# Six plain units for nine in a gated product, eight decoded blocks in the experts, and a ranking matmul placed later

## The chip, the cores and the metric

The kernel runs on one core of one Trainium2 chip. The time is the device time of one launch in microseconds (us). A core has a tensor engine (TensorE, PE), three engines for elementwise work (VectorE = DVE, ScalarE = ACT, GpSimd = POOL), an engine that issues most DMA transfers (SyncE, SP), and 16 DMA engines. Each engine works through a list of its own in order; semaphores tie the lists together.

## The reference

Three layers in a row, on 4 x 576 = 2304 tokens of 512 numbers:

```python
# 1: causal attention, 4 batches x 8 heads, 576 tokens, head dim 64
scores = q @ k.T / 8;  cum = cumsum(max(s, 0))
scores = where(causal, -1e9, scores + min(-(cum_i - cum_j), 0))
x = softmax(scores) @ v                    # -> [2304, 512]
# 2: mixture of experts, one expert for each token, D = 512, F = 1024, E = 8
expert_idx = argmax(x @ w_gate, 1);  gate_w = softmax prob of that expert
out[mask] = gate_w[mask, None] * (max(x[mask] @ w1[e], 0) @ w2[e])
# 3: RMS norm and a gated product, d_ff = 1536
xn = x / sqrt(mean(x * x) + 1e-6) * rms_g
g = xn @ w_gate;  y = (g * sigmoid(g) * (xn @ w_val)) @ w_out
```

The inputs w_gate, w_val and w_out of the third layer arrive as 64-bit numbers, all others as fp32.

## The kernel before

**Order.** PE, ACT, DVE and SP run their instructions in the order in which the program writes them. So what is written ahead of an instruction on the same engine also holds it up.

**Attention.** 16 pairs of heads, written by a plan of times (ten to a pair). For each batch `route(b)` scores the tokens, picks their experts and ranks them within their expert, as a generator that is advanced a step at a time between the pieces of attention. Its ranking matmuls (L509, L511: the triangle `tri` and the ones against the one-hot matrix `oh`, which DVE makes at L503) are put off by a number of steps for each batch, `(3, 10, 3, 0)[b]`. The tokens are then scattered to DRAM (`xs`) by GpSimd, ordered by expert.

**Experts.** `moe` runs experts 0 to 7. Expert 0 begins while the last batch is still being ranked: its first 256 rows go through `gemm1` and `gemm2` as transposed tiles; 128 rows more, the late rows `xl`, are loaded, multiplied by their gate weight (`gate`, L867 on ACT), turned by PE (`turn_tile`, `xq`, L894) and go through `rows_gemm1` (L973) and `rows_gemm2` (L984). Then `finish` norms the rows, and PE turns the late rows' result (`yt`, L1001). Weights come in pieces of 512 KB: `feed` takes the next item of the list `k.order` and issues its load on SP (L729) into a ring of four staging buffers; `split` takes the oldest loaded piece, makes its upper part on ACT (L744) and its remainder on DVE (L757), and feeds the next item. The list holds 56 pieces (experts 1 to 7, eight each) and, at every ninth place from 12 on, five *words*: blocks of 512 KB of 64-bit numbers, three of w_out and one each of w_gate and w_val. `decode_words` turns a word into fp32: two steps on DVE (L1239, L1240), the absolute value on ACT, then two more steps on DVE, then a store to DRAM on SP (`keep_words`, L786: `wo32`, `wg32`) and the feed of the next item. One word is decoded in each of experts 1 to 5, its first half behind column 0 of `gemm2`, its second half ahead of the add of column 1.

**Gated product.** 36 units (p, f): a pair of token groups p of 3 and a block f of 12 of the width 1536. A unit is a 2 x 2 block product. The plain units (`PLAIN`, nine of them: f = 0, 1, 2 for each p) use eight products of blocks; the other 27 use seven, with sums of the x blocks (`x_sum`, S1 to S4), sums of the weight blocks (`w_sum`) and more steps at the eviction (STEPS7 against STEPS8). A product is six matmuls of 384 columns (L1314, 2 halves x 3 passes of upper parts and remainders). All of it is written by times in units of a product: `SLOTS_V` and `SLOTS_G` are places on DVE and POOL, `fill` takes the next free one, `x_rests`, `x_sums`, `w_made` and `w_split` place the making of x and weight blocks. `glu_head` loads the first blocks during the last expert; the fp32 words of f = 0 are read back into `k.flat`. The second product (with w_out) follows.

```python
for n, item in enumerate(words):
    k.order.insert(WORDS_AT + 9 * n, item)
...
gemm2(k, 0, 1, NA)
rank(1)
gate(k, k.xl, ((0, 128),))
gemm2(k, 0, 2, NA)
...
turn_tile(k, k.xl[:, 0, :], *xb)
```

## Time and profile before

| | value |
|---|---|
| three timed runs, us | 848.29, 848.42, 849.98 (median 848.42) |
| profiled execution, us | 841.21, its span 839.5 |
| PE busy | 818.7 us, 98% |
| PE weight loads (beside PE) | 748.2 us, 89% |
| DVE busy | 640.0 us, 76% |
| ACT busy | 462.7 us, 55% |
| POOL busy | 226.5 us, 27% |
| granted clock of PE, mean | 0.994 |
| DMA | 146.72 MB, 175 GB/s |

On PE the stages lie thus in the span: attention to 184 us (the first `gemm1` matmul), the experts to 416 (the first of L1314), the gated product to 691, the second product to 828. On the other engines they overlap. Busy times are of one profiled execution, whose own time is 7.2 us below the median of the timed runs. A busy share is a mean over stages with different limits, so what an engine costs is read from who waits for whom in a stage.

### The profile page before, as it was taken

Reading aid. Unit: us, or ns where it says so; the run is one execution under the profiler, and the core shown is the slowest. Engines: PE = TensorE matmul, PEld = TensorE weight load, DVE = VectorE, ACT = ScalarE, POOL = GpSimd, SP = SyncE. Lnnn points to the kernel's source line nnn. Section 1 sums busy time; section 2 is a strip of 40 time slices with the busy share of each in tenths; the row PEclk is TensorE's granted clock in tenths of the full one; section 3 lists DMA queues with packets and bytes.
Section 4 is the critical chain, followed back from the end, with each engine's and each line's share of the span. In section 5 each row is a group of like instructions: output and inputs, shape, how many; then the busy total and the mean of one; then the engine's idle time right before and its main releaser. Section 6 shows DMA issues by size and latency. Waiting matters only on the chain.

```text
span 839.5 us, 15787 instructions
## 1 busy us (share of the span) xinstructions
PE 818.7 (98%) x5622; PEld 748.2 (89%) x5622; DVE 640.0 (76%) x1425; ACT 462.7 (55%) x1060; POOL 226.5 (27%) x249
## 2 busy tenths in 40 slices
PE   7999999999999999999999999999999999999994
PEld 4777767789899999999999999999999998899994
DVE  6557688965767767867698988888898969868880
ACT  5988988875756566566453443333333335453440
POOL 3335845342000000000131232544343352032120
PEclk9999999999999999999999999999999999999997
DMA  7999978246567576767651433323233375344510
GB/s 226 301 317 304 320 245 270 101 133 203 182 200 247 182 226 198 230 224 219 239 197 48 148 104 107 111 104 107 88 107 107 108 280 173 99 151 145 158 52 30
DMA packets 79757, 146.72 MB, mean 175 GB/s; under 512 B 7424, under 2 KB 44315, under 8 KB 79667
## 3 DMA queue, kind: packets, MB, share of 16 engines
q1 hardware_dynamic: 76707, 136.08, 51.1%
q0 software_dynamic: 2912, 9.46, 3.0%
q8 instruction: 46, 0.75, 0.4%
q14 instruction: 44, 0.36, 0.1%
q10 hardware_dynamic: 48, 0.07, 0.0%
HBM read 108.04 MB, written 37.54 MB: 173 GB/s over the span
## 4 chain that ended last, share of the span: by engine, by line
PE 92%; DVE 3%; ACT 1%; DMA 1%; issue 1%; SPq 0%; POOL 0%; POOLq 0%; ACTq 0%; DVEq 0%
PE gg L1314 29%; PE g L935 12%; PE g L912 12%; PE gp L1772 10%; PE go L1707 6%; PE t L370 5%; PE s L307 5%; PE pvy L416 5%; PE tl L444 2%; PE sm L338 2%; PE xp L883 1%; DMA ringa<-ytd 1%; PE r L984 1%; PE r L973 1%; ACT pt L403 0%
## 5 line engine op out<-in xcount | busy, mean ns | idle before, releaser
L935 PE MATMUL g<-h,u 128*128 128x256 f32 (+7 forms) x768 | 105.0, 295 | 0.0
L912 PE MATMUL g<-xt,u 128*128 128x256 f32 (+7 forms) x768 | 104.2, 295 | 0.0
L912 PEld LDWEIGHTS g<-xt,u 128*128 128x128 f32 x768 | 101.4, 189 | 0.8
L935 PEld LDWEIGHTS g<-h,u 128*128 128x128 f32 x768 | 101.2, 189 | 0.5
L1291 POOL TENSOR_TENSOR ws<-raw,ws 128x512 fp32r<-128x512 f32 (+1 forms) x25 | 33.0, 1335 | 220.4 <-ACT ws L1286 220.4
L744 ACT CAST u<-raw 128x1024 fp32r<-128x1024 f32 x62 | 65.1, 1050 | 19.5 <-DMA raw<-in_w 19.5
L351 ACT ACTIVATE p<-sc,nm 128x128 f32<-128x128 f32 (+3 forms) x128 | 71.3, 582 | 6.8 <-DVE nm L295 6.8
L757 DVE TENSOR_TENSOR u<-raw,u 128x1024 fp32r<-128x1024 f32 x58 | 70.5, 1218 | 0.4 <-ACT u L744 0.4
L1314 PE MATMUL gg<-gx2a,ws 128*128 128x384 f32 x360 | 67.4, 336 | 0.6 <-DVE tmp L1336 0.6
L1314 PE MATMUL gg<-gx0a,ws 128*128 128x384 f32 x360 | 67.7, 336 | 0.0
L1314 PE MATMUL gg<-gx1a,ws 128*128 128x384 f32 x360 | 67.1, 335 | 0.0
L1314 PEld LDWEIGHTS gg<-gx2a,ws 128*128 128x128 f32 x360 | 62.8, 188 | 0.9 <-DVE tmp L1336 0.9
L1314 PEld LDWEIGHTS gg<-gx0a,ws 128*128 128x128 f32 x360 | 63.1, 188 | 0.0
L1314 PEld LDWEIGHTS gg<-gx1a,ws 128*128 128x128 f32 x360 | 62.7, 188 | 0.0
L1352 POOL TENSOR_TENSOR hs<-tmp,hs 128x384 f32<-128x384 f32 x27 | 30.2, 1120 | 106.3 <-ACT hs L1350 106.3
L403 ACT COPY pt<-t 128x512 f32<-128x512 f32 (+3 forms) x160 | 56.1, 454 | 3.1 <-PE t L370 2.0
L370 PE MATMUL t<-ident,p 128*128 128x128 f32 x400 | 52.2, 275 | 0.0
L370 PEld LDWEIGHTS t<-ident,p 128*128 128x128 f32 x400 | 44.5, 140 | 8.4 <-DVE nm L295 8.3
L1693 POOL DMA_INDIRECT out<-raw,oid x18 | 20.5, 1139 | 111.9 <-DVE raw L1794 64.5
L416 PE MATMUL pvy<-pt,vp 128*64 128x512 f32 (+4 forms) x320 | 47.5, 428 | 0.7 <-ACT pt L403 0.7
L1332 ACT COPY tmp<-gg 128x384 f32<-128x384 f32 x27 | 13.0, 481 | 57.2 <-PE gg L1314 55.5
L1242 ACT ACTIVATE raw<-raw 128x512 f32<-128x512 f32 x31 | 21.2, 682 | 36.0 <-DVE raw L1240 35.9
(391 smaller groups left out, 1812.3 us busy)
## 6 DMA issues: line engine op xcount, KB each, us to landing
raw<-in_w SPq DMA_DIRECT2D x64, 512.0 KB
hd<-hs SPq DMA_DIRECT2D x72, 192.0 KB
xs<-zrow SPq DMA_DIRECT2D x8, 771.0 KB
raw<-in_wo SPq DMA_DIRECT2D x12, 512.0 KB
raw<-in_wg SPq DMA_DIRECT2D x12, 512.0 KB
raw<-in_wv SPq DMA_DIRECT2D x12, 512.0 KB
vp<-in_v SPq DMA_DIRECT2D x16, 320.0 KB
in<-cumd SPq DMA_DIRECT2D x20, 256.0 KB
```

What stands on the lines that cost most here:

```text
L307: k.nc.tensor.matmul(ps[h], st.q[r, 128 * i:128 * i + 128], st.k[r, 0:w], start=True, stop=p >= BYPE)
L351: k.nc.scalar.activation(out, st.s[i, h][:, 0:w], AF.Exp, bias=st.nm[:, n:n + 1], scale=-1.0, accum_out=acc)
L370: nc.tensor.transpose(ps[:, off:off + 128], src[:, 128 * j:128 * j + 128], k.ident)
L403: nc.scalar.copy(b, a)
L416: nc.tensor.matmul(st.y[r, a - 64:512], st.v[:, h, j, :], k.pt[:, h, o:o + S - a], start=j == 0, stop=j == 4)
L744: nc.scalar.copy(w[:, :, 0, :], raw)
L757: k.nc.vector.tensor_tensor(w[:, :, 1, :], raw, w[:, :, 0, :].bitcast(F32), op=ALU.subtract)
L912: nc.tensor.matmul(ps[:, 0:n], w[:, f % 4, a, 128 * kc:128 * kc + 128], x[b][:, kc, 0:n], start=kc == 0 and i == 0, stop=kc == 3 and i == 2)
L935: nc.tensor.matmul(ps[:, 0:n], w[:, f % 4, a, 128 * c:128 * c + 128], k.h[b][:, f, 0:n], start=f == 0 and i == 0, stop=f == 7 and i == 2)
L1314: k.nc.tensor.matmul(k.ps[u, bank], w[:, a, 128 * c:128 * c + 128], x[:, b, GT * c:GT * c + GT], start=first and c == 0 and n == 0, stop=c ...
L1707: k.nc.tensor.matmul(k.acc[tau], c[:, a, 128 * t:128 * t + 128], w[:, b, :], start=f == 0 and i == 0, stop=f == NF - 1 and i == 2)
L1772: k.nc.tensor.matmul(k.acc[i, bank], t[:, a, j, :], item_weight(k, j, w, b), start=first and j == 0 and n == 0, stop=j == 5 and n == 2, sk ...
```

## The change

- **Plain units.** `PLAIN` loses (0, 2), (1, 2) and (2, 2): six units with eight products, thirty with seven. The places on DVE and POOL are made anew from `UNITS`. The S sums of p = 0 and p = 1 stand earlier in the plan, the blocks f = 2 get weight sums.
- **Words.** Eight are decoded in the experts: three of w_out, one each of w_gate and w_val for f = 0 and for f = 2, and the one of w_gate for f = 3 (`WORDS`). `wg32` has room for four blocks; `words_load` reads them back, and f = 2 is no longer decoded in the gated product, f = 3 only half. The string `PIECES_AND_WORDS` gives the order of pieces (p) and words (w) in `k.order`: the words stand at the first and the fourth place, both used up in expert 0, and then, behind ten items, at the fifth place in each of six groups of nine. In expert 0, `decode_words` begins ahead of the gate of `xl` and ends behind column 2 of `gemm2`; a second one begins ahead of column 3 and ends behind it.
- **Ranking.** The matmuls of batch 0 are put off by 10 steps rather than 3, those of batch 1 by 18 rather than 10; `RSTEPS` grows to 56.

```diff
@@ route
-    for _ in range((3, 10, 3, 0)[b]):
+    for _ in range((10, 18, 3, 0)[b]):
         yield 1
...
-RSTEPS = 47
+RSTEPS = 56
@@ keep_words
-    out = k.wo32[f // 2 - 2][:, f % 2, :] if m == 2 else k.wg32[:, m, :]
+    out = k.wo32[f // 2 - 2][:, f % 2, :] if m == 2 else k.wg32[f][:, m, :]
@@ moe
-    k.order = [(s, u, q) for s in range(1, E) for u in range(4) for q in (0, 2)]
-    words = [(E, 2, f) for f in range(4 + EARLY_OUT, NF)] + [(E, 0, 0), (E, 1, 0)]
-    for n, item in enumerate(words):
-        k.order.insert(WORDS_AT + 9 * n, item)
-    chain = iter(())
+    pieces = [(s, u, q) for s in range(1, E) for u in range(4) for q in (0, 2)]
+    words = [(E, 2, f) for f in range(4 + EARLY_OUT, NF)] + [(E, m, f) for f, n in WORDS.items() for m in range(n)]
+    k.order, chain = [(words if c == "w" else pieces).pop(0) for c in PIECES_AND_WORDS], iter(())
...
     gemm2(k, 0, 1, NA)
     rank(1)
+    chain = decode_words(k)
+    next(chain)
     gate(k, k.xl, ((0, 128),))
     gemm2(k, 0, 2, NA)
+    next(chain)
...
     split(k)
     gate(k, k.x[1], first)
     split(k)
+    chain = decode_words(k)
+    next(chain)
     gemm2(k, 0, 3, NA)
+    next(chain)
     split(k)
...
-            if c == 0 and s <= len(words):
+            if c in (0, 2) and k.staged and k.staged[0][0] == E:
                 chain = decode_words(k)
                 next(chain)
...
-WORDS_AT = 6 + 6
+WORDS = {0: 2, 2: 2, 3: 1}
+PIECES_AND_WORDS = "wppwpppp" + "pp" + 6 * ("ppp" + "pwpppp")
...
-PLAIN = ((0, 0), (0, 1), (1, 0), (1, 1), (2, 0), (2, 1), (0, 2), (1, 2), (2, 2))
-UNITS = (list(PLAIN) + [(p, f) for f in range(3, NF - 2) for p in range(3)]
+PLAIN = ((0, 0), (0, 1), (1, 0), (1, 1), (2, 0), (2, 1))
+UNITS = (list(PLAIN) + [(p, f) for f in range(2, NF - 2) for p in range(3)]
@@ new
+def words_load(k, f):
+    k.val[f] = staging(k, [2, 512], F32)
+    n = WORDS[f]
+    k.nc.sync.dma_start(out=k.val[f][:, 0:n, :], in_=k.wg32[f][:, 0:n, :])
@@ glu_head
-    k.flat = staging(k, [2, 512], F32)
-    k.nc.sync.dma_start(out=k.flat, in_=k.wg32)
+    words_load(k, 0)
...
+    words_load(k, 2)
@@ w_made
-        for m in range(2):
-            add(load[f] + 0.1 * m, w_load, k, f, m)
-        for n in range(8):
-            t = fill(load[f] + 6.0)
-            add(t, w_decode, k, f, n)
-        for n in range(0 if whole else 4):
+        t = load[f] + 4.0
+        if f > 2:
...
+            for n in (2, 3, 6, 7) if f in WORDS else range(8):
+                t = fill(load[f] + 6.0)
+                add(t, w_decode, k, f, n)
+        for n in range(2 * (f == 2), 4):
             t = fill(t)
             add(t, w_sum, k, f, n)
@@ glu, the order of the x blocks
-    x_rests(1, (("A11", V), ("A12", V), ("A21", V), ("A22", G)), 8.1)
...
-    w_made(2)
-    x_rests(2, (("A11", V), ("A12", G), ("A21", V), ("A22", V)), 19.0)
-    w_split(2)
-    w_made(3)
-    x_sums(0, ("S3", "S1", "S2", "S4"), 12.5)
-    x_rests(0, (("S2", G), ("S3", V), ("S4", V)), 12.0)
...
+    x_sums(0, ("S3", "S1", "S2", "S4"), 1.0)
+    x_rests(0, (("S2", G),), 1.0)
+    x_rests(1, (("A11", V), ("A12", V), ("A21", V), ("A22", G)), 7.0)
+    x_rests(0, (("S3", V), ("S4", V)), 12.0)
+    x_rests(0, (("S1", V),), START[LAST[0]] + A21_AT)
...
+    x_rests(2, (("A11", V), ("A12", G), ("A21", V), ("A22", V)), 18.0)
...
+    x_sums(1, ("S3", "S1", "S2", "S4"), 18.0)
+    x_rests(1, (("S2", G), ("S3", V), ("S4", V)), 18.0)
+    w_made(2)
...
+    w_split(2)
+    x_sums(2, ("S3", "S1", "S2", "S4"), done[0, "S1"] + 8.0)
+    x_rests(2, (("S2", V), ("S3", G), ("S4", V), ("S1", V)), START[LAST[2]] + A21_AT)
+    w_made(3)
+    w_split(3)
```

**ACT in expert 0**, where the late rows are gated: `y` and `sq` are the copy and the square of a column of `gemm2` (`g`), `xl` is the gate, `xb` the copy of the turned late rows, `raw` a staging buffer. Before:

```order
L937 COPY y_2903<-g_1_2943 128x256
L942 ACTIVATE sq_2904<-g_1_2943 128x256
L867 ACTIVATE xl<-xl 128x512
L937 COPY y_2903<-g_2_2985 128x256
L942 ACTIVATE sq_2904<-g_2_2985 128x256
L896 CAST xb_3013<-xq_3015 128x4x128
```

Now:

```order
L937 COPY y_2903<-g_1_2943 128x256
L942 ACTIVATE sq_2904<-g_1_2943 128x256
L1247 ACTIVATE raw_2897<-raw_2897 128x512
L867 ACTIVATE xl<-xl 128x512
L937 COPY y_2903<-g_2_2988 128x256
L942 ACTIVATE sq_2904<-g_2_2988 128x256
L896 CAST xb_3021<-xq_3023 128x4x128
```

The absolute value of the first word stands between column 1 and the gate of `xl`.

**SP in expert 0**, from the first item of `k.order`: `raw` are staging buffers, `wo` is the DRAM of decoded w_out blocks, `nb` a read of token counts, `tokd` the expert order of the tokens. Before:

```order
L729 DMA raw_2897<-in_w 128x1024
L729 ISA
L729 DMA raw_2899<-in_w 128x1024
L729 ISA
L729 DMA raw_2901<-in_w 128x1024
L805 TENSOR_LOAD nb
L862 REGISTER_ALU
L862 DMA tokd<-ids_3022 1x128
L729 ISA
L729 DMA raw_3032<-in_w 128x1024
L729 ISA
L729 DMA raw_3039<-in_w 128x1024
```

Now:

```order
L1231 DMA raw_2897<-in_wo 128x1024
L729 ISA
L729 DMA raw_2899<-in_w 128x1024
L729 ISA
L729 DMA raw_2901<-in_w 128x1024
L786 DMA wo_66<-raw_2897 128x512
L1231 DMA raw_3019<-in_wo 128x1024
L805 TENSOR_LOAD nb
L862 REGISTER_ALU
L862 DMA tokd<-ids_3030 1x128
L729 ISA
L729 DMA raw_3040<-in_w 128x1024
```

A word has taken the first place; its store and the next word's load stand ahead of the count and the ids. (Four rows behind the last, the store of the second word, `wo_66<-raw_3019`, stands ahead of the load of the fifth piece.)

**PE at the ranking of batch 1** (`rk`): `pvy` are the value products of a pair of heads, `s` the scores of the next group. Before:

```order
L416 MATMUL pvy_1747<-pt_152,vp_147 64x448 x2
L416 MATMUL pvy_1747<-pt_152,vp_147 64x320 x2
L416 MATMUL pvy_1747<-pt_152,vp_147 64x192 x2
L509 LDWEIGHTS tri
L509 MATMUL rk_1764<-oh_1716,tri 128x40
L511 LDWEIGHTS ones
L511 MATMUL rk_1764<-oh_1716,ones 128x32
```

Now:

```order
L416 MATMUL pvy_1747<-pt_152,vp_147 64x64 x2
L307 MATMUL s_0_0_1769<-in_141 128x128
L307 MATMUL s_0_1_1770<-in_141 128x128
L307 MATMUL s_1_0_1778<-in_141 128x256
L307 MATMUL s_1_1_1779<-in_141 128x256
L307 MATMUL s_3_0_1793<-in_141 128x512
L307 MATMUL s_3_1_1794<-in_141 128x512
L307 MATMUL s_2_0_1801<-in_141 128x384
L307 MATMUL s_2_1_1802<-in_141 128x384
L509 LDWEIGHTS tri
L509 MATMUL rk_1814<-oh_1716,tri 128x40
L511 LDWEIGHTS ones
```

One value product and the eight score matmuls of the next group stand ahead of the first `rk` matmul.

## Rows read from the trace of the kernel before

**Rows 1.** The chain that ended last, by engine: share of the span.

```profile
PE 92%; DVE 3%; ACT 1%; DMA 1%; issue 1%; SPq 0%; POOL 0%; POOLq 0%; ACTq 0%; DVEq 0%
```

**Rows 2.** Waits: engine, line waited for; us in total, times, longest us.

```profile
PE rk L509 <- DVE oh L503: 1.6, 2, 1.4
...
PEld L509 <- DVE oh L503: 3.1, 3, 1.7
```

**Rows 3.** The chain in order of time: start and length, us.

```profile
418.89 64.50 PE gg L1314 x372
```

**Rows 4.** DVE's groups, 424 to 467 us: us busy, mean ns | idle before.

```profile
L1217 DVE TENSOR_TENSOR gx2a<-gx2b,gx2a 128x768 fp32r<-128x768 f32 x3 | 3.8, 1307 | 0.2 <-ACT gx2a L1211 0.2
L1206 DVE TENSOR_TENSOR ringa<-ringa 128x768 f32<-128x768 f32 x4 | 3.8, 954 | 0.1
...
L1346 DVE TENSOR_TENSOR hs<-gg,hs 128x384 f32<-128x384 f32 x6 | 3.3, 550 | 0.9 <-ACT hs L1344 0.8
```

**Rows 5.** PE's timeline in expert 0: start, length in us; in brackets its wait.

```profile
204.32 0.60 PE L894 MATMUL xq<-ident,xl 128*128 128x128 f32 x4
...
216.76 5.85 PE L984 MATMUL r<-u,hb 128*128 128x512 f32 x24
...
224.70 0.66 PE L1001 MATMUL yt<-ident,hr 128*128 128x128 f32 x4 [0.36 <-ACT hr L994]
```

**Rows 6.** ACT's timeline, at four places.

```profile
202.25 0.73 ACT L867 ACTIVATE xl<-xl 128x512 f32<-128x512 f32 x1
...
209.69 0.37 ACT L942 ACTIVATE sq<-g 128x256 f32<-128x256 f32 x1
...
216.45 1.06 ACT L744 CAST u<-raw 128x1024 fp32r<-128x1024 f32 x1
...
252.62 1.05 ACT L744 CAST u<-raw 128x1024 fp32r<-128x1024 f32 x1 [2.14 <-DMA raw<-in_w]
...
412.15 0.68 ACT L1242 ACTIVATE raw<-raw 128x512 f32<-128x512 f32 x1
```

**Rows 7.** DVE's timeline, expert 0 and a word's first steps.

```profile
204.02 0.14 DVE L608 TENSOR_SCALAR nb<-nb 1x1 uint32<-1x1 uint32 x1
...
210.43 2.35 DVE L757 TENSOR_TENSOR u<-raw,u 128x1024 fp32r<-128x1024 f32 x2
...
219.33 1.75 DVE L960 RECIPROCAL sq<-sq 128x256 f32<-128x256 f32 x1 [0.78 <-ACT sq L959]
221.12 1.67 DVE L963 SCALAR_TENSOR_TENSOR y<-y,gv,sq 128x256 f32<-128x256 f32 x4
223.76 0.16 DVE L993 RECIPROCAL ss<-ss 128x1 f32<-128x1 f32 x1 [0.97 <-ACT ss L992]
...
410.47 0.42 DVE L1239 TENSOR_SCALAR raw<-raw 128x512 uint32<-128x512 uint32 x1
410.93 0.70 DVE L1240 SCALAR_TENSOR_TENSOR raw<-raw 128x512 uint32<-128x512 uint32 x1
```

**Rows 8.** SP's queue in order of time: when issued.

```profile
200.82 1.53 SPq L729 DMA_DIRECT2D raw<-in_w  x3
...
247.83 0.33 SPq L786 DMA_DIRECT2D wo<-raw  x1
248.43 4.30 SPq L729 DMA_DIRECT2D raw<-in_w  x4
```

**Rows 9.** All transfers into staging buffers (tile raw).

```profile
DMA to landing us min/median/max: 2.7/4.4/7.8
```

**Rows 10.** Stretches at the end: engines' busy us, PE's clock, DMA share, GB/s.

```profile
827.00:828.00 1.00, 0.65 (x6) 0.44 (x4) 0.32 (x1) 0.00 (x0) 0.32 (x1) 1.00 0.24 74
830.00:831.00 1.00, 0.00 (x0) 0.00 (x0) 0.00 (x0) 0.00 (x0) 0.00 (x0) 0.51 0.64 233
```

**Rows 11.** PE's timeline at the start of attention.

```profile
12.80 1.93 PE L338 MATMUL sm<-in 128*128 128x288 f32 x4
...
20.41 1.14 PE L338 MATMUL sm<-in,p 128*128 128x288 f32 x4
```

More of the change, by code (lines that the diff above doesn't have):

```diff
@@ L1014, in rank @@
             next(k.last, None)
-    k.order = [(s, u, q) for s in range(1, E) for u in range(4) for q in (0, 2)]
-    words = [(E, 2, f) for f in range(4 + EARLY_OUT, NF)] + [(E, 0, 0), (E, 1, 0)]
-    for n, item in enumerate(words):
-        k.order.insert(WORDS_AT + 9 * n, item)
-    chain = iter(())
+    pieces = [(s, u, q) for s in range(1, E) for u in range(4) for q in (0, 2)]
+    words = [(E, 2, f) for f in range(4 + EARLY_OUT, NF)] + [(E, m, f) for f, n in WORDS.items() for m in range(n)]
+    k.order, chain = [(words if c == "w" else pieces).pop(0) for c in PIECES_AND_WORDS], iter(())
+    assert not pieces and not words
     row = ids(k, k.x[0], EARLY)
@@ L1135 @@
 WHENS = ((0, 1, 4, 5, 6, 9, 10), (0, 1, 6, 4, 5, 7, 8))
[L1136 to L1140 removed]
+START = [sum(7 + (x in PLAIN) for x in UNITS[0:u]) for u in range(len(UNITS) + 1)]
+SLOTS_V = [START[u] + o for u, x in enumerate(UNITS) for o in (
+    (0.65, 1.2, 1.75, 2.2, 3.25, 4.65, 5.2, 5.75, 6.25, 7.25) if x in PLAIN else (1.3, 1.9, 2.5, 3.65, 4.15))]
+SLOTS_G = [START[u] + o for u, x in enumerate(UNITS) for o in ((0.2, 2.2, 4.2, 6.2) if x in PLAIN else (0.05, 1.6))]
 STEPS7 = (("u1", 1.05), ("gate1", 5.7), ("u2", 4.6), ("sig1", 5.05), ("u3", 7.1), ("c22", 7.65), ("c21", 10.1),
@@ L1262, in w_parts @@
 def w_parts(k, f):
-    if f == 0:
-        return k.flat[:, 0, :], None, k.flat[:, 1, :], None
+    if f == 3:
+        v, raw = k.val[f], k.raw[f, 1].bitcast(F32)
+        return v[:, 0, :], v[:, 1, :], raw[:, :, 1], raw[:, :, 0]
+    if f in WORDS:
+        v, t = k.val[f], k.scr.get(f)
+        return (v[:, 0, :], t and t[:, 0, :], v[:, 1, :], t and t[:, 1, :])
     return [k.raw[f, m].bitcast(F32)[:, :, n] for m in range(2) for n in (1, 0)]
 def w_sum(k, f, n):
+    if f == 2 and n == 0:
+        k.scr[f] = staging(k, [2, 512], F32)
     g, gl, v, vl = w_parts(k, f)
@@ L1305, in glu_product @@
     p, f = UNITS[u]
-    whole = u < len(PLAIN)
+    whole = (p, f) in PLAIN
     bank, xi, wi = (WHOLE if whole else SEVEN)[j]
@@ L1322, in glu_step @@
     add, mult = ALU.add, ALU.mult
-    whole = u < len(PLAIN)
+    whole = (p, f) in PLAIN
     if whole:
@@ L1421, in glu @@
         last[f] = u
-        whole = u < len(PLAIN)
+        whole = (p, f) in PLAIN
         when = range(8) if whole else WHENS[u == len(UNITS) - 1]
@@ L1467, in glu @@
         add(8.0 + 0.1 * g, glu_load, k, g)
-    x_rests(1, (("A11", V), ("A12", V), ("A21", V), ("A22", G)), 8.1)
     load, over, sent = {2: 0.5, 3: 6.5}, {}, {}
     def w_made(f):
-        whole = (0, f) in PLAIN
-        for m in range(2):
-            add(load[f] + 0.1 * m, w_load, k, f, m)
-        for n in range(8):
-            t = fill(load[f] + 6.0)
-            add(t, w_decode, k, f, n)
-        for n in range(0 if whole else 4):
+        t = load[f] + 4.0
+        if f > 2:
+            for m in range(2):
+                if m < WORDS.get(f, 0):
+                    add(load[f] + 0.1 * m, words_load, k, f)
+                else:
+                    add(load[f] + 0.1 * m, w_load, k, f, m)
+            for n in (2, 3, 6, 7) if f in WORDS else range(8):
+                t = fill(load[f] + 6.0)
+                add(t, w_decode, k, f, n)
+        for n in range(2 * (f == 2), 4):
             t = fill(t)
@@ L1483, in w_split @@
     def w_split(f):
-        whole = (0, f) in PLAIN
         end = last[f - 2] + 1
@@ L1487, in w_split @@
         t = v = at
-        for n, eng in ((0, V), (4, G), (1, V)) if whole else ((0, V), (2, G), (3, G), (1, V)):
+        for n, eng in ((0, V), (2, G), (3, G), (1, V)):
             if eng is V:
```

32 lines of the change are left out of this document (12 added, 20 removed).

## The prediction

> **What bounds the kernel now.** I read the chain that ended last first. TensorE (PE) carries 92% of it [rows 1], so a change moves the end by what it takes from PE, or by what it makes PE wait for. Then I read what PE waits for: apart from the start, the longest wait is at the two matmuls that rank tokens, 1.6 us together [rows 2]. The other engines are off the chain, but in two stages they stand close behind it: VectorE (DVE) at the start of the gated product, and in expert 0 a short chain through ScalarE (ACT) on which PE takes rows that were gated just before [rows 5, 6].
>
> **The change part by part.**
>
> Six plain units for nine. Three units (block 2 for the three token pairs) go from eight products to seven. A product is 6 matmuls, so 18 matmuls of 384 columns go. The chain shows 372 of them in 64.50 us [rows 3], 0.173 us each: 18 x 0.173 = **3.1 us less**, all on PE, which has no gap there. What the seven-product form wants in exchange (sums, three evictions more per unit) is on DVE and ACT, and is hidden only if DVE keeps up. By the order, DVE has between the last expert's norm and unit 6: 24 gate instructions, 11 sums of x, 14 remainders of x, and 7 short ones. At 0.55, 0.954, and 0.954 to 1.307 us [rows 4], with 0.5 for the short ones: 13.2 + 10.5 + (13.4 to 18.3) + 3.5 = 41 to 46 us. The norm is over some 7 products in, so there are 41 products of 1.04 us, 43 us. DVE is full, and by the upper end 3 us late. But unit 6 itself reads blocks that stand early in that list; the last of it, the p = 2 blocks, is first read in unit 8, at product 61, 13 us later. I take 0, and keep 0 to 3 us of new waits as a range.
>
> The decoded words in experts 1 to 6. One per expert as before in experts 1 to 5 and one new in expert 6; there the order stands as in expert 5, in which PE did not wait. 0, cover being the free time of DVE and ACT; if that were gone it would cost the two instruction pairs on DVE, about 2.4 us [rows 7].
>
> The ranking. The 0.6 us or so of ranking matmuls stay; the waits go. In batch 1 the whole score group now stands ahead of them (third order piece), 2.4 us of PE work against a longest wait of 1.4; in batch 0 one value product moves ahead of a wait of 0.3. That gives **1.6 us less**. The upper bound is 3.1, what the weight load of these matmuls waits for in all three batches [rows 2]. I take the 1.6, since PE's own idle time is what can be won. The scatters that follow come a little later on GpSimd; nothing reads them before the early tokens are loaded, tens of us on.
>
> The two words in expert 0. Here the order shows new waits. ACT and DVE run their lists in order, and so does the queue of SyncE (SP).
>
> First word. ACT now has the absolute value of the word ahead of the gate of the late rows, and PE's transposes (xq) of these rows stand right behind gemm2's third column. Before, the gate ran from 202.25 to 203.0 and PE took the rows without a wait at 204.32 [rows 5, 6]. Now: the word has the place of the first weight piece in SP's queue, issued at 200.8 [rows 8]; with the median of 4.4 us from issue to landing [rows 9] it is there at 205.2. DVE comes free of the ranking list at 204.2 [rows 7], so it waits, then needs 1.2 us for two steps (410.47 to 411.63), ACT 0.7 for the absolute value and 0.7 for the gate: 205.2 + 1.2 + 0.7 + 0.7 = 207.8. PE's xq starts 3.5 us late. A word that has landed in time still leaves 204.2 + 2.6 = 206.8, that is 2.5 us late; this floor needs no DMA at all.
>
> Second word. SP's store of the first word waits for its last two DVE steps (207.1 + 1.2 = 208.3), and the second word's load is queued behind that store. The nearest rows for such a pair are in expert 1: store at 247.83, next load at 248.43, ACT waits for it until 252.62 [rows 6, 8], 4.8 us after the store. So the second word is there at 213.1. Then 1.2 (DVE), 0.7 (ACT), 0.6 for copy and square of the fourth column, 0.4 for the add, 1.2 for a weight remainder (half of the pair at 210.43) and 1.2 for the last steps [rows 6, 7]: 218.4.
>
> Behind it. The second store holds up the load of the fifth piece for expert 1 in the same way: there at 218.4 + 4.8 = 223.2, where before it was long there. Its cast stands on ACT ahead of the square root of expert 0's norm, and the norm stands on DVE ahead of the small reciprocal (L993) on which the row scale, and then PE's yt, wait. From that cast to the norm's reciprocal it was 219.33 - 216.45 = 2.9 us, from there to the norm's end 222.8 - 219.33 = 3.5, and from L993 to yt 224.70 - 223.76 = 0.9 [rows 5 to 7]: 223.2 + 7.3 = 230.5. PE's own work, shifted by the 3.5 above, would be there at 228.2, so a second wait of 2.3 us opens, and yt is **5.8 us late** against 224.70. PE is without gaps from there to the gated product, so nothing gives this back.
>
> Bounds: 2.5 (all transfers at the shortest landing, 2.7 us [rows 9]; then yt is held by nothing but the first wait) and, with each of the three transfers 1 us slower than taken, 8.8; all three at the longest 7.8 us would be far more, which I leave out, as one such among many is rare.
>
> The Trainium skill, "DMA: Bandwidth & Descriptors", section "Anatomy of one DMA", gives about 2.0 us plus bytes over 436 GB/s; for these 512 KB that is an estimate of 3.2 us, below the median row here. By it the first word would be there before DVE is, and the loss in expert 0 some 2.5 to 3 us, not 5.8; the row decides, since other transfers are queued ahead here.
>
> Sum: -3.1 - 1.6 + 5.8 = **+1.1 us**. The profiled execution took 841.2 us (span 839.5, 1.7 around it), so the changed kernel would take 842.3 there. The timed runs lie 7.2 us higher (median 848.42); the difference carried over gives **849.5**.
>
> **The rivals.**
>
> (B) Slower: the gap in expert 0 costs more than its wait. Either each transfer comes 1 us later (loss 8.8, net +4.1, 852.5), or PE's clock falls in the gap. For the clock the trace has this: after the last matmul, at 827.65, the granted clock is down to 0.51 in the stretch from 830 [rows 10], so an idle PE fell from 2.4 to 1.2 GHz in under 3 us; and at the start, out of a wait, the same four matmuls took 1.93 us against 1.14 later [rows 11]. A gap of 3.5 us is longer than that. The price is half the time spent at the lower level; if that is 4 to 8 us, 2 to 4 us, of which the 2.3 us wait at yt absorbs the first part, since that wait is set by DMA, ACT and DVE. So it decides only if PE at half rate loses more than 2.3 us: net +1.1 to +2.8, up to 851.2. The Trainium skill, "TensorE: Matmul & The Clock Gate", section "Why this matters for your kernels", speaks against this change in the same sense: idle gaps between bursts of matmuls bring the lower clock. The trace agrees at its end.
>
> (C) Faster: the loads land early. For it: the shortest landing is 2.7 us, and the first word only has to be there by 204.2. Then the loss is the floor of 2.5, net -2.2, **846.2**. Against: 0.6 MB of expert rows are queued ahead of that word, and the pair in expert 1 took 4.8.
>
> (D) DVE too late in the first product: 3 us of waits at units 6 to 8 on top of the forecast, net +4.1, 852.5. It decides once DVE is more than 13 us behind unit 6, or if the x blocks of units 2 and 3 slip by over 2 us. Against: DVE also loses four decode pairs there.
>
> That the change does not do what it says can be ruled out: the order shows the matmuls gone and the ranking moved.
>
> **How the numbers follow.** This kernel's measurement can tell 0.2%, 1.7 us, from no change. Forecast (loss in expert 0 between 4.3 and 6.4, time 848.0 to 850.1): 0.48. B: 0.23. C: 0.17. D: 0.12. The likeliest time is the forecast's 849.5. C gives faster nearly whole, 0.16. Slower is B, most of D and the upper edge of the forecast: 0.23 + 0.09 + 0.03 = 0.35. The rest, 0.49, is the same. The range takes in C's floor and B's upper case: 846.0 to 852.5.
>
> **What would show it.** Matmuls of the gated product down by 18; the wait of rk on oh gone. In expert 0, PE idle before xq (L894) of 2.5 to 4 us with ACT's gate as its releaser, and before yt (L1001) of about 2 us with hr behind it; SP's stores of the words waiting for DVE. If xq shows under 2 us, my reading of ACT's order is wrong; if yt shows nothing, the DMA price was too high and C holds; a granted clock under 1 in that stretch is B; new waits on DVE in units 2, 3 or 6 to 8 are D.

## The result and the profile after

The changed kernel takes 859.83 us (median of four runs, 859.04 to 860.75) against 848.36 for the kernel before: ratio 1.0131, 95% interval 1.0114 to 1.0149, **11.5 us slower**. Forecast were 849.5 us, within 0.2%, and a range up to 852.5. The direction of the sum was right, its size was not. Its profiled execution took 859.64 us with a span of 857.9.

PE's share of the chain that ended last fell from 92% [rows 1] to 77%. Part 4 of the page after:

```profile
PE 77%; DVE 7%; DMA 7%; ACT 4%; issue 2%; another core or an unknown queue 1%; POOL 1%; SPq 0%; POOLq 0%; DVEq 0%; ACTq 0%
```

The other answer is in what PE waits for (the list of waits, PE alone; us in total, times, longest):

```profile
PE s L307 <- DMA in<-in_k: 5.2, 1, 5.2
PE xq L894 <- ACT xl L867: 5.0, 1, 5.0
...
PE xq L894 <- ACT hr L975: 1.7, 1, 1.7
PE gg L1331 <- DVE tmp L1351: 1.5, 3, 0.6
PE ms L957 <- DVE sq L943: 1.4, 1, 1.4
PE g L935 <- DVE h L916: 1.2, 1, 1.2
...
PE yt L1001 <- ACT hr L994: 0.4, 1, 0.4
```

The waits of `rk` [rows 2] are gone, as forecast. The first line is the start of attention (5.2 us before as well). The largest of the others is new: `xq`, the turning of the late rows, waits 5.0 us. The wait forecast at `yt` isn't there in this trace (0.4 us, as in rows 5); another stands at the `xq` of `hr`. A second trace of the same kernel (after_again) has it at `yt`:

```profile
PE xq L894 <- ACT xl L867: 5.5, 1, 5.5
...
PE yt L1001 <- ACT hr L994: 0.8, 1, 0.8
...
PE xq L894 <- ACT hr L975: 0.5, 1, 0.5
```

To find the stage, I read the starts of four groups of matmuls in PE's timeline: the first `gemm1`, `yt`, the first `gg` (gated product), the first `go` (second product), and the end of the last matmul. In the trace of after:

```profile
190.09 2.14 PE L912 MATMUL g<-xt,u 128*128 128x256 f32 x16
...
240.94 0.66 PE L1001 MATMUL yt<-ident,hr 128*128 128x128 f32 x4 [0.36 <-ACT hr L994]
...
436.58 2.27 PE L1331 MATMUL gg<-gx0a,ws 128*128 128x384 f32 x12
...
709.70 2.49 PE L1731 MATMUL go<-gx1a,ringa 128*128 128x512 f32 x10
...
846.74 0.51 PE L1796 MATMUL gp<-ws,ringa 128*128 128x256 f32 x3
```

The same differences for every trace (us), and the timed ratio to before with its interval. The kernel before was timed anew in each job, that is, beside each group of kernels, and the ratio is within a job:

| kernel | attention, to first gemm1 | expert 0, to yt | experts, yt to gg | gated product | second product | ratio to before |
|---|---|---|---|---|---|---|
| before | 184.2 | 40.5 | 191.5 | 275.0 | 136.4 | 1 |
| before_again | 188.4 | 41.0 | 191.5 | 275.4 | 136.4 | - |
| **after** | 190.1 | **50.9** | **195.6** | **273.1** | 137.6 | 1.0131 [1.0114, 1.0149] |
| after_again | 190.0 | 49.5 | 194.7 | 273.1 | 137.7 | 1.0136 [1.0108, 1.0163] |
| rank_only | 193.0 | 40.5 | 191.5 | 275.0 | 136.4 | 1.0011 [0.9998, 1.0023] |
| no_rank | 190.4 | 49.6 | 196.2 | 273.2 | 136.5 | 1.0097 [1.0080, 1.0114] |
| seven_words | 192.5 | 48.7 | 191.5 | (273.4) | 136.5 | 1.0057 [1.0041, 1.0072] |
| six_words | 184.3 | 40.6 | 194.2 | 273.9 | 136.5 | 1.0001 [0.9990, 1.0012] |
| moved_words | 185.5 | 40.5 | 209.8 | 273.1 | 136.5 | 1.0156 [1.0141, 1.0171] |
| gate_first | 183.2 | 50.2 | 194.8 | 273.1 | 136.4 | 1.0096 [1.0070, 1.0122] |
| pool_store | 184.2 | 46.9 | 193.6 | 273.2 | 136.5 | 1.0052 [1.0036, 1.0067] |
| moved_pool | 190.3 | 40.6 | 208.2 | 273.9 | 137.6 | 1.0166 [1.0149, 1.0184] |
| early_pool | 191.4 | 47.0 | 193.7 | 273.9 | 137.6 | 1.0078 [1.0056, 1.0100] |
| load_only | 190.4 | 40.5 | 192.2 | 274.0 | 136.4 | 0.9977 [0.9966, 0.9989] |
| f_words | 189.0 | 40.6 | 195.2 | 273.2 | 136.9 | 1.0027 [1.0011, 1.0043] |
| f_words_pool | 191.0 | 40.5 | 195.0 | 274.1 | 136.4 | 1.0023 [1.0009, 1.0037] |
| late_words | 192.1 | 40.9 | 194.7 | 273.6 | 136.8 | 1.0033 [1.0007, 1.0059] |
| late_old | 191.1 | 41.7 | 195.0 | 274.1 | 137.9 | 1.0026 [1.0013, 1.0040] |

Against the first trace of before: expert 0 +10.3, the other experts +4.1, the gated product -1.9, the second product +1.1, and attention +5.9. Attention is no clean difference: before_again, the same kernel as before, was 4.2 us later there than its first trace. The second product takes 136.4 to 136.9 us, or 137.6 to 137.9 in the five traces in which its matmuls (`gp`) wait 0.8 or 0.9 us for DVE; kernels that are alike there stand on either side, so its 1.1 is no part of the change either. The 841.2 us from which the prediction set out was an execution with a short attention: before_again took 5.2 us more, 4.2 of them there. That the 7.2 us between it and the timed runs lie mostly there is likely, but the timed runs left no traces.

**Expert 0.** PE's, ACT's, DVE's and SP's timelines of after, in this order (start and length in us, the wait in brackets):

```profile
215.42 1.06 PE L894 MATMUL xq<-ident,xl 128*128 128x128 f32 x4 [5.00 <-ACT xl L867]
...
216.35 4.24 PE L935 MATMUL g<-h,u 128*128 128x256 f32 x24
...
227.83 0.66 PE L894 MATMUL xq<-ident,hr 128*128 128x128 f32 x4 [1.67 <-ACT hr L975]
```

```profile
214.10 0.65 ACT L1247 ACTIVATE raw<-raw 128x512 f32<-128x512 f32 x1 [5.81 <-DVE raw L1245]
214.66 0.71 ACT L867 ACTIVATE xl<-xl 128x512 f32<-128x512 f32 x1
...
226.24 1.05 ACT L744 CAST u<-raw 128x1024 fp32r<-128x1024 f32 x1 [1.94 <-DMA raw<-in_w]
227.19 0.59 ACT L975 ACTIVATE hr<-r 128x512 f32<-128x512 f32 x1
```

```profile
209.96 0.14 DVE L608 TENSOR_SCALAR nb<-nb 1x1 uint32<-1x1 uint32 x1
212.87 0.43 DVE L1244 TENSOR_SCALAR raw<-raw 128x512 uint32<-128x512 uint32 x1 [2.77 <-DMA raw<-in_wo]
...
215.94 0.42 DVE L943 TENSOR_TENSOR sq<-sq 128x256 f32<-128x256 f32 x1 [1.92 <-ACT sq L942]
216.28 0.42 DVE L1248 TENSOR_SCALAR raw<-raw 128x512 f32<-128x512 f32 x1
```

```profile
207.87 0.35 SPq L1231 DMA_DIRECT2D raw<-in_wo  x1
...
217.46 0.33 SPq L786 DMA_DIRECT2D wo<-raw  x1
...
219.84 0.94 SPq L729 DMA_DIRECT2D raw<-in_w  x2
226.98 0.33 SPq L786 DMA_DIRECT2D wo<-raw  x1
```

Read it from the bottom: the word's load is issued at 207.87, DVE is through with the ranking list at 210.1 and waits 2.77 us for the word; ACT waits 5.81 us for DVE; the gate, which in rows 6 ran at once, stands behind that and PE waits 5.0 us. The first store (217.46) is late besides, because the word's last two steps on DVE (from 216.28) stand behind the add of column 2 (L943), which waits for the gate, the copy and the square on ACT. The second stall of this trace has another door than I thought: at 226.24 a cast waits for pieces that were issued at 219.84, behind that store, and behind the cast on ACT stands the eviction of `hr` (L975), which PE needs 13 us ahead of `yt`. And PE ran slow behind each stall, as the table of stretches shows (the stretch and its length, the busy us of PE, its weight loads, DVE, ACT and POOL, then PE's granted clock):

```profile
210.00:220.00 10.00, 5.00 (x30) 4.71 (x29) 4.50 (x8) 5.28 (x11) 0.00 (x0) 0.83 0.62 213
220.00:230.00 10.00, 8.26 (x43) 6.55 (x43) 5.22 (x8) 5.96 (x12) 0.00 (x0) 0.96 0.63 196
230.00:240.00 10.00, 10.00 (x47) 7.84 (x46) 7.21 (x12) 5.73 (x12) 0.00 (x0) 0.87 0.52 176
```

The mean is below 1 behind both stalls: part of each stretch ran at 1.2 GHz, half of the 2.4 before (granted 0.50 from 216 to 218 and from 230 to 232). The 24 matmuls of `gemm2` at 216.35 took 4.24 us; in before the same 24 took 3.06:

```profile
204.78 3.06 PE L935 MATMUL g<-h,u 128*128 128x256 f32 x24
```

With `xq` (1.06 for 0.60 [rows 5]) and the small matmuls from 229 on, PE's work took about 3 us longer at the lower clock.

Four traces have this expert 0, and their second stall is not at one place (waits of PE, and what expert 0 takes over before's 40.5, us):

| trace | `xq` of `xl` | `xq` of `hr` | `yt` | expert 0 |
|---|---|---|---|---|
| after | 5.0 | 1.7 | 0.4 | +10.3 |
| after_again | 5.5 | 0.5 | 0.8 | +9.0 |
| no_rank | 5.4 | none | 1.4 | +9.0 |
| seven_words | 4.8 | none | 1.1 | +8.2 |

In the last three `yt` waits on the path that was forecast. ACT's and PE's timelines of after_again:

```profile
232.37 1.05 ACT L744 CAST u<-raw 128x1024 fp32r<-128x1024 f32 x1 [1.23 <-DMA raw<-in_w]
...
238.81 0.69 ACT L994 ACTIVATE hr<-r,ss 128x512 f32<-128x512 f32 x1 [0.66 <-DVE ss L993]
```

```profile
239.55 0.65 PE L1001 MATMUL yt<-ident,hr 128*128 128x128 f32 x4 [0.79 <-ACT hr L994]
```

The cast waits for the piece that was issued behind the second store, the square root and DVE's norm stand behind it, and the small reciprocal (L993) behind the norm holds the row scale. In after DVE's norm also ended late, at 238.8; on that path alone `yt` would have been some 9.1 us late (an estimate: PE's rows came 1.2 us after the norm). So this path makes `yt` 8.2 to 9.1 us late in all four traces, and in after the stall at `hr` with the slow matmuls behind it added about 1.2 us.

**The last expert.** ACT's, SP's and PE's timelines of after, around the sixth word's store:

```profile
412.11 1.05 ACT L744 CAST u<-raw 128x1024 fp32r<-128x1024 f32 x1 [3.67 <-DMA raw<-in_w]
...
415.65 1.05 ACT L744 CAST u<-raw 128x1024 fp32r<-128x1024 f32 x1 [1.91 <-DMA raw<-in_w]
416.60 0.63 ACT L915 ACTIVATE h<-g 128x248 fp32r<-128x248 f32 x2
```

```profile
407.21 0.33 SPq L786 DMA_DIRECT2D wg<-raw  x1
407.81 1.62 SPq L729 DMA_DIRECT2D raw<-in_w  x2
```

```profile
414.26 0.72 PE L957 MATMUL ms<-sq,ones 128*128 128x268 f32 x2 [1.38 <-DVE sq L943]
...
427.63 9.11 PE L935 MATMUL g<-h,u 128*128 128x248 f32 x77 [1.19 <-DVE h L916]
```

Two weight pieces are issued behind the store, and ACT waits 3.67 and 1.91 us for them. Behind these casts stand a column's square (L942, for which `sq` waits), the square root ahead of DVE's norm, and the relu evictions of the last expert (L915 on ACT, L916 on DVE), and PE runs dry twice. The two gaps are 2.6 of the 4.1 us; the granted clock stayed at 1.00 here.

### The profile page after: what moved, and what is told of

It is laid out like the page before. It is cut to its first block, busy times and chain, and to the rows that moved or that the text cites. A ratio compares the mean times of both kernels' runs of the same rounds, so it can differ in the third digit from the quotient of the medians.

```text
span 857.9 us, 15778 instructions
## 1 busy us (share of the span) xinstructions
PE 823.4 (96%) x5604; PEld 748.7 (87%) x5604; DVE 647.1 (75%) x1438; ACT 462.0 (54%) x1064; POOL 238.2 (28%) x256
## 4 chain that ended last, share of the span: by engine, by line
PE 77%; DVE 7%; DMA 7%; ACT 4%; issue 2%; another core or an unknown queue 1%; POOL 1%; SPq 0%; POOLq 0%; DVEq 0%; ACTq 0%
PE gg L1331 27%; PE gp L1796 9%; PE g L912 9%; PE g L935 9%; PE go L1731 6%; PE s L307 4%; PE pvy L416 4%; PE t L370 4%; DMA in<-cumd 2%; DMA raw<-in_w 2%; PE tl L444 2%; PE sm L338 1%; PE xp L883 1%; ACT u L744 1%; DMA x<-xs 1%
## 5 line engine op out<-in xcount | busy, mean ns | idle before, releaser
L935 PE MATMUL g<-h,u 128*128 128x256 f32 (+7 forms) x768 | 107.3, 298 | 1.3 <-DVE h L916 1.2
L1308 POOL TENSOR_TENSOR ws<-raw,ws 128x512 fp32r<-128x512 f32 (+1 forms) x26 | 35.7, 1392 | 228.0 <-ACT ws L1303 225.7
L1369 POOL TENSOR_TENSOR hs<-tmp,hs 128x384 f32<-128x384 f32 x30 | 34.2, 1141 | 121.1 <-ACT hs L1367 121.1
L1331 PE MATMUL gg<-gx2a,ws 128*128 128x384 f32 x336 | 63.8, 336 | 0.6 <-DVE tmp L1353 0.6
L1331 PE MATMUL gg<-gx0a,ws 128*128 128x384 f32 x336 | 63.9, 336 | 0.0
L1331 PE MATMUL gg<-gx1a,ws 128*128 128x384 f32 x336 | 63.2, 335 | 0.0
L1331 PEld LDWEIGHTS gg<-gx2a,ws 128*128 128x128 f32 x336 | 58.6, 188 | 0.9 <-DVE tmp L1353 0.9
L1331 PEld LDWEIGHTS gg<-gx0a,ws 128*128 128x128 f32 x336 | 59.0, 188 | 0.0
L1331 PEld LDWEIGHTS gg<-gx1a,ws 128*128 128x128 f32 x336 | 58.6, 188 | 0.0
```

Source lines behind the costliest of these rows:

```text
L935: nc.tensor.matmul(ps[:, 0:n], w[:, f % 4, a, 128 * c:128 * c + 128], k.h[b][:, f, 0:n], start=f == 0 and i == 0, stop=f == 7 and i == 2)
L1308: eng.tensor_tensor(w[:, c, LO, :], src, plain(w[:, c, HI, :]), op=ALU.subtract)
L1331: k.nc.tensor.matmul(k.ps[u, bank], w[:, a, 128 * c:128 * c + 128], x[:, b, GT * c:GT * c + GT], start=first and c == 0 and n == 0, stop=c ...
```

## The experiments

Theory after the result: a word costs because three in-order queues wait for it, DVE for its landing, ACT for DVE, SP's store for DVE's last steps, and what stands behind (the gate, `hr`, relu evictions, later pieces) is late. Rivals: the moved ranking made the rows late; the word's place in the staging ring; execution-to-execution variation.

**before_again**, **after_again**: both kernels unchanged, traced once more.

> The kernel before, unchanged, with a second trace. Its first profiled execution took 841.2 us, its four timed ones 848.2 to 850.0, and the profiled execution of the changed kernel reached the first gemm1 matmul 5.9 us later than that of before. Theory A (attention varies from execution to execution): this trace reaches the first gemm1 matmul at 188 to 191 us and takes about 848 us, with waits on loads of the bias or after the scatters. Theory B (the moved ranking made attention late): it is there at 184 us again, and the 7 us between the first profile and the timed runs lie elsewhere.

846.4 us, first gemm1 at 188.4. Theory A, though 188.4 is only just within its bounds and the time is 1.6 us below its 848: attention varies, and the stages behind it agree within 0.5 us.

> The changed kernel, unchanged. Theory (the losses are fixed by the order): 9.5 to 11 us more than before's 40.5 from the first gemm1 matmul to yt, 3.5 to 5 more than its 191.5 from yt to the gated product, 1.5 to 2.5 less than its 275.0 in the gated product; 10 to 12 us slower than before. Rival (they vary as the transfers do): one of the stretches off by 3 us or more from these.

859.73 against 848.82. Expert 0 +9.0, a little under the stated bound, the experts +3.2, also a little under, the gated product -1.9. The losses come again, each a microsecond smaller, with the second wait of expert 0 mostly at `yt`.

**rank_only**, **no_rank**: one part alone, and one part undone.

```diff
-    for _ in range((3, 10, 3, 0)[b]):
+    for _ in range((10, 18, 3, 0)[b]):
...
-RSTEPS = 47
+RSTEPS = 56
```

> The kernel before with the ranking alone moved (steps 10 and 18 for 3 and 10). My prediction: 1.6 us faster than before, about 846.8. Rival (the scatters of GpSimd that follow the ranking now stand behind other GpSimd work, and PE waits for scores to be taken in the pair after them, about 3 us in batch 0 and 1.3 us in batch 1): 3 to 5 us slower, 851 to 853. Third: within 0.8 us of before.

> The changed kernel with the ranking put back (steps 3 and 10). By my prediction 1.6 us slower than the changed kernel, 861.4. By the rival 3 to 5 us faster, 855 to 857. If the order of ranking costs nothing, 859.8, and the first gemm1 matmul comes no earlier than in the changed kernel's trace (190.1 us).

rank_only against before, the waits of PE in attention (before_again first, then rank_only, from the same job):

```profile
PE rk L509 <- DVE oh L503: 1.4, 1, 1.4
PE s L307 <- ACT vp L428: 1.1, 1, 1.1
```

```profile
PE s L307 <- ACT vp L428: 2.8, 2, 1.7
...
PE sm L338 <- DVE base L533: 0.5, 1, 0.5
```

The 1.4 us at `rk` go and 2.2 us come (1.7 more at `s`, 0.5 at `sm`, whose mask now stands behind the later ranking steps on DVE). Behind the 1.7 us wait at `s`, at 138.5, the granted clock is 0.50 for some 6 us. Timed, rank_only is 1.0011 of before, interval 0.9998 to 1.0023: no gain, and the forecast's 0.2% gain lies outside. no_rank is 0.3% nearer to before than the changed kernel, but the two were timed in different jobs, its expert 0 and experts are about as slow as in after's two traces, 1.1 us of its gap is the second product, and late_old against late_words (below), in one job, shows no difference. So no gain shows, and a loss of up to 0.2% isn't ruled out; the rival's 3 to 5 us fell too.

**six_words**: no word in expert 0; two blocks of w_out are left out of the computation.

```diff
...
-    chain = decode_words(k)
-    next(chain)
     gate(k, k.xl, ((0, 128),))
     gemm2(k, 0, 2, NA)
-    next(chain)
...
-PIECES_AND_WORDS = "wppwpppp" + "pp" + 6 * ("ppp" + "pwpppp")
+PIECES_AND_WORDS = "pppppppp" + 6 * ("ppp" + "pwpppp")
```

> The changed kernel with no word in expert 0: two of the three w_out blocks are not decoded, and the third one's numbers are stored in their places as well (so two blocks of the second product are left out of the computation). Expert 6 keeps its word. It measures the price of expert 0's two words: in the traces the stretch from the first gemm1 matmul to yt is 10.3 us longer with them than before. Theory (the whole 10.3 us is those two words): the stretch is 40.5 us again and the time falls by 9 to 11 us against the changed kernel, to 1 to 2 us above before. Rival (half of it is the moved ranking, whose scatters make the rows of expert 0 late): the stretch stays at 44 us or more and the time falls by 5 or less.

Expert 0 is back at 40.6 and the ratio at 1.0001, 11 us below the changed kernel. All of the 10.3 us is those two words.

**seven_words**: no word in expert 6.

```diff
-WORDS = {0: 2, 2: 2, 3: 1}
+WORDS = {0: 2, 2: 2}
-PIECES_AND_WORDS = "wppwpppp" + "pp" + 6 * ("ppp" + "pwpppp")
+PIECES_AND_WORDS = "wppwpppp" + "pp" + 5 * ("ppp" + "pwpppp") + "pppppppp"
```

> The changed kernel without the word in expert 6: the block of w_gate for f = 3 is decoded in the gated product instead (two more instruction pairs on DVE there). In the changed kernel the gated product begins 4.1 us later behind expert 0's end than before, with ACT waiting 3.7 and 1.9 us for two weight pieces that were issued behind the store of that word. Theory (the sixth word costs the last expert its pieces): 3.5 to 4.5 us faster than the changed kernel, 855.3 to 856.3. Rival (the loads for the gated product, words_load, make the pieces late, not the word): under 1 us. Third (DVE has no room for the pairs in the gated product): gains 4 and loses 2 or more there.

With four more instructions on DVE the plan writes the weights of block 3 behind the first product that reads them, so this product takes older numbers, and its stage is not read here. The stretch ahead of it, yt to gg, is 191.5, as before: the 4.1 us are the sixth word.

**gate_first**, **pool_store**, **early_pool**: three ways around the waits in expert 0. gate_first writes the word's decode behind the late rows' turning; pool_store issues the stores on GpSimd; early_pool adds to that an early load.

```diff
@@ gate_first
-    chain = decode_words(k)
-    next(chain)
     gate(k, k.xl, ((0, 128),))
...
     keep_ids(k, row, column(k, 1))
+    chain = decode_words(k)
+    next(chain)
+    next(chain)
     split(k)
@@ pool_store
-    keep_words(k, m, f, raw)
+    keep_words(k, m, f, raw, k.nc.gpsimd)
@@ early_pool, besides
         if f == 3:
+            feed(k)
             load_late(k)
...
-    feed(k, STG - 1)
+    feed(k, STG - 2)
...
     gemm2(k, 0, 0, NA)
     rank(1)
+    chain = decode_words(k)
+    next(chain)
     gemm2(k, 0, 1, NA)
     rank(1)
-    chain = decode_words(k)
-    next(chain)
```

> The changed kernel with the first word's decode behind the gate and the turning of the late rows instead of ahead of them, the second word as it is. Theory (the gate behind the word's absolute value on ACT is what PE waits for): the wait of xq on xl, 5 us, goes, and the half clock behind it, 1.6 us, so the time is 5 to 7 us below the changed kernel; the wait of xq on hr stays or grows to 2 to 3 us, since the second word comes as late as before. Rival (the word's load is late anyway, so the wait moves to the next thing behind it on ACT, the copy of xb or the casts): under 2.5 us gained.

> The changed kernel with the stores of the decoded words issued by GpSimd instead of SP, so that no load stands behind a store that waits for DVE. Theory (SP's order makes the later pieces late): the wait of xq on hr in expert 0 (1.7 us) and the 4.1 us in the last expert mostly go, 3 to 6 us below the changed kernel; the wait of xq on xl, 5 us, stays. Rival (the ring of four buffers holds the loads, not the store ahead of them): under 1 us gained.

> pool_store with the first word of expert 0 loaded ahead of the late rows (its load is issued at gemm1 column 3, some 10 us earlier) and its first steps written behind column 0 of gemm2 instead of just ahead of the gate. Theory (xq waits for that word's landing and the steps behind it): the wait of xq on xl, 3.7 us in pool_store, goes, and the half clock behind it (2.4 us more between xq and the next xq than before); 41 to 42.5 us from the first gemm1 to yt, 4.5 to 6 us faster than pool_store, within 0.2% of before. Rival (with the word gone from there, the second word or a piece is what ACT waits for next): the wait turns up at the xq of hr, and under 3 us are gained.

gate_first: the wait of `xq` on `xl` is gone and expert 0 takes 50.2 us all the same. (Timed, its ratio of 1.0096 is 8 us, 3 less than its stages behind attention add up to; without a trace of before from its job that stays open.) PE's and ACT's timelines of gate_first:

```profile
219.14 1.12 PE L894 MATMUL xq<-ident,hr 128*128 128x128 f32 x4 [6.70 <-ACT hr L975]
```

```profile
216.46 0.65 ACT L1247 ACTIVATE raw<-raw 128x512 f32<-128x512 f32 x1 [5.53 <-DVE raw L1245]
...
217.54 1.04 ACT L744 CAST u<-raw 128x1024 fp32r<-128x1024 f32 x1
218.48 0.61 ACT L975 ACTIVATE hr<-r 128x512 f32<-128x512 f32 x1
```

ACT's list still has the second word, a column's copy and square, a cast and then `hr`; the wait at `xl`, moved away, came back at `hr` as a wait for the second word. The rival was right in kind: the next thing on ACT waits. pool_store: 46.9, 4 us better (2.6 against after_again), with the `hr` wait gone and 2.1 of the 4.1 us in the last expert too, so SP's order was part of it. early_pool: the wait on `xl` goes as planned, but 47.0 stays, now as two waits of `xq` on `hr` (1.7 and 1.6 us) with casts that wait 1.73, 1.17 and 1.38 us for pieces. Again the rival, and the stated 4.5 us did not come.

**moved_words**, **moved_pool**, **load_only**: all eight words outside experts 0 and 6. moved_pool is moved_words with pool_store's edit; load_only leaves three blocks out of the computation.

```diff
@@ moved_words, besides six_words' lines of expert 0
-PIECES_AND_WORDS = "wppwpppp" + "pp" + 6 * ("ppp" + "pwpppp")
+PIECES_AND_WORDS = "pppppppp" + 3 * ("ppppwpppwp") + 2 * ("ppppwpppp") + "pppppppp"
@@ load_only, besides, for the second word of an expert
-    for step in decoding(k, raw)[0:3]:
-        step()
+    if not skip:
+        for step in decoding(k, raw)[0:3]:
+            step()
```

> The changed kernel, all eight words decoded, in other places: none in expert 0 and none in expert 6, two in each of experts 1 to 3 (at columns 0 and 2 of gemm2) and one in each of experts 4 and 5. Theory (the place costs, not the number): expert 0 loses nothing, 40.5 us from gemm1 to yt, 191.5 from yt to the gated product as before, and only the gated product's gain of about 2 us is left: 1 to 2 us faster than before if the ranking is neutral, 0 to 1 slower if it costs 1 to 2. Rival (a second word in any expert holds up the pieces behind its store, as the sixth did): 2 to 4 us lost in each of experts 1 to 3, 6 to 12 us slower than that.

> The words where moved_words has them (two in each of experts 1 to 3, one in experts 4 and 5), their stores issued by GpSimd instead of SP. In moved_words each expert with two words took 6.1 us longer, with ACT waiting 2.8 us for a piece that was issued behind the store, and 2.6 us for DVE's steps on the second word. Theory S (SP's order: the store holds up the pieces behind it): under 2 us for each of the three, so 12 us or more faster than moved_words, about the time of before. Theory R (the ring of four buffers: a word takes a piece's buffer until it is stored): 4 us or more for each stays, at most 6 us faster than moved_words.

> moved_words with the second word of experts 1 to 3 loaded and taken from the ring, but neither decoded nor stored; in its place the first word of that expert is stored twice (so three blocks of w_out, w_gate and w_gate are left out of the computation). In moved_words the stretch from yt to the gated product was 18.3 us longer than before. Ring theory (a word takes a buffer and a landing, so the pieces behind it come late): 12 us or more of the 18.3 stay. Theory of the steps (DVE's and ACT's steps on the word, and the store, stand ahead of casts and relu evictions): 6 us or less stay.

moved_words fell on its rival's side: expert 0 is clean (40.5), and the other experts take 18.3 us more, 6.1 for each second word. With the stores on GpSimd 16.7 of it stay, so SP's order is not the main part. DVE's timeline of moved_pool at the first second word, which ACT waits 4.0 us for:

```profile
260.78 0.43 DVE L1238 TENSOR_SCALAR raw<-raw 128x512 uint32<-128x512 uint32 x1 [2.37 <-DMA raw<-in_wo]
```

That speaks for either theory then left, the ring or the waiting steps. load_only tells them apart as far as it goes: the same loads through the same ring, nothing decoded, and only 0.7 of the 18.3 us stay. So the transfers alone cost little; what costs is decoding a word that has just landed, with the buffer held meanwhile. (How much of it is the held buffer and how much the engines' waiting isn't separated.) Its ratio, 0.9977, is what six plain units bring with three words' decode left out and the first word's store written twice in place of theirs.

**f_words**, **f_words_pool**, **late_words**, **late_old**: the second word where pieces are taken slowly.

```diff
@@ f_words
-3 * ("ppppwpppwp") + 2 * ("ppppwpppp")
+3 * ("pppwpwpppp") + 2 * ("ppppwpppp")
...
+            if f == 6 and k.staged and k.staged[0][0] == E:
+                chain = decode_words(k)
+                next(chain)
+            elif f == 7:
+                next(chain, None)
@@ late_words, against f_words
-3 * ("pppwpwpppp") + 2 * ("ppppwpppp")
+"ppppwpppp" + 3 * ("pppwpwpppp") + "ppppwpppp"
...
-            if f == 6 and k.staged and k.staged[0][0] == E:
+            if f == 7 and k.staged and k.staged[0][0] == E:
                 chain = decode_words(k)
                 next(chain)
-            elif f == 7:
-                next(chain, None)
```

f_words_pool is f_words with pool_store's edit, late_old is late_words with the ranking of before.

> moved_words with the second word of experts 1 to 3 decoded behind columns 6 and 7 of gemm1 instead of behind columns 2 and 3 of gemm2; all eight words are decoded. Theory (the word must stand where pieces are taken from the ring at long distances): the stretch from yt to the gated product is within 3 us of before (194.5 or less against 209.8 in moved_words), 15 us faster than moved_words, and with the gated product's 1.9 us the whole within 0.3% of before, at best 2 us faster. Rival (any second word costs an expert its 6 us): the stretch stays over 205 us.

> f_words with the stores of the words issued by GpSimd. Theory (once the ring is not the limit, what stands behind the store on SP is): another 0 to 3 us faster than f_words, and 1 to 2 us faster than before. Rival: no change against f_words.

> f_words with the second word of an expert one column later (its first steps behind column 7 of gemm1, behind all relu evictions, its last steps behind column 0 of gemm2), and in experts 2 to 4 instead of 1 to 3. In f_words the three second words cost 3.7 us, 2.1 of it in expert 1. Theory (what costs is an engine that waits in order for a word that has not landed): from yt to the gated product 191.5 to 192.5 us, the whole 1 to 2 us faster than before if the ranking is neutral. Rival (a second word's steps cost 0.7 us an expert by themselves): 193.5 or more, within 0.2% of before.

> late_words with the ranking put back to steps 3 and 10. If the moved ranking is neutral: as late_words within 0.8 us. If it costs what rank_only showed (0.1%): 0.9 us faster than late_words. By my prediction's reading 1.6 us slower.

f_words: the second words cost 3.7 us instead of 18.3, so the place is most of the price; a little more than the 3 us stated. The stores on GpSimd add nothing there (195.0). late_words: 194.7, its rival's side: a second word costs about 1 us even so, and the whole came out a little worse than the 0.2% stated (1.0033). In late_old PE's timeline shows where:

```profile
324.49 0.74 PE L957 MATMUL ms<-sq,ones 128*128 128x300 f32 x2 [0.91 <-DVE sq L943]
...
354.84 0.73 PE L957 MATMUL ms<-sq,ones 128*128 128x292 f32 x2 [1.76 <-DVE sq L943]
```

The norm's matmul waits in two experts one after the other, as in after's last expert. Of the versions that decode all eight words, f_words_pool is the nearest to before, and it is slower (1.0023, interval 1.0009 to 1.0037). None beats the kernel before.

## Why the prediction was wrong, point by point

Two steps failed most: the path through expert 0, priced at 5.8 us, took 8.2 to 10.3, and the words in experts 1 to 6, put at 0, took 3.2 to 4.7. Of the 4.7 us that were to be won, 1.9 came.

- **Six plain units, -3.1 us**: -1.9 measured, in both traces of the changed kernel (-0.9 to -1.9 in the others with this plan). The 18 matmuls are gone; the stage's waits for `tmp` grew by 1.0 us, from three to four, each of up to 0.65 us. PE waited for no x block at units 6 to 8, so rival D did not happen, but "I take 0" for the added evictions was mis-sized by that microsecond.
- **Ranking, -1.6 us**: -0.2 to +1.9 by rank_only's interval. The step that failed is "PE's own idle time is what can be won". The wait at `rk` went, and PE then waited later in attention; a wait on the path is a gain only if nothing else is due right behind it. Why PE waits for `vp` there isn't settled: it shows in most traces with either order, but neither in before's first trace nor in the four of one job (six_words, moved_words, gate_first, pool_store). These five are also the traces with the short attention (183 to 185.5 us, the others 188 to 193).
- **First word, 3.5 us**: mechanism and place right, 5.0 measured (4.8 to 5.5 in the four traces). The load was issued 1.1 us later than I took (207.87, against 200.82 plus attention's 5.9), and landed after 5.0 us, not 4.4.
- **Second word and fifth piece, yt 5.8 us late**: the path was right, its length was not. Beside the first word's 1.7 us, the step that failed is "SP's store of the first word waits for its last two DVE steps", taken right behind the absolute value: on DVE the add of column 2 stands ahead of them, 1.5 us that I left out. So the first store came 3.2 us late (217.46, against 208.3 plus 5.9), and the second word, the second store and the fifth piece were 2.7 to 3.4 us late behind it; `yt` was 9.0 us late in after_again, not 5.8. What the path missed is the cast ahead of `hr` (L975), whose piece stands behind the first store: in after it cost PE 1.7 us, in after_again 0.5, in no_rank and seven_words nothing.
- **The clock**: named in rival B, and priced as absorbed by the wait at `yt`. In three of the four traces `yt` still waited, 0.4 to 1.1 us longer than before, so there the slow matmuls were hidden, as B's pricing had it; in after they and the stall at `hr` came to about 1.2 us more than the path. Along PE's own list the 10.3 us of after read 5.0 + 1.7 of waits and some 3.5 more, most of it at the lower clock. One of B's signs does not hold: in before the granted clock is shown as 1.00 from 8 to 22 us, so the 1.93 us of rows 11 are no evidence of it.
- **Words in experts 1 to 6, 0 us**: wrong by 4.1 (3.2 in the second trace, 4.7 in no_rank), all of it the sixth word in expert 6. "The order stands as in expert 5" was true of the order, not of the time: rows 6 showed ACT already waiting 2.14 us for a piece behind a word's store, and I read PE's silence as room. Why expert 6 bears such a wait worse than experts 1 to 5 isn't separated.
- The Trainium skill, "DMA: Bandwidth & Descriptors", section "Anatomy of one DMA — SWDGE (gpsimd) path", gives its sum for transfers that GpSimd issues; these are issued by SP, so the estimate of 3.2 us was taken from the wrong path. The load took 5.0 us here, and the measurement decides.
- The same Trainium skill's "TensorE: Matmul & The Clock Gate", section "Why this matters for your kernels", says that idle gaps between bursts of matmuls bring the lower clock. The trace agrees behind the 5.0 us gap (granted clock 0.50 from 216 to 218).

With the measured terms the sum is -1.9 + 0 + 10.3 + 4.1 = +12.5, and -1.9 + 0 + 9.0 + 3.2 = +10.3 by the second trace; the timed runs, +11.5, lie between.
